# An RWKV-5 attention with a SoLU layer behind it: merged products from the fifth chunk on, and five smaller moves

## Chip, cores and metric

One core of a Trainium2 chip runs the program. Its engines are TensorE (PE, with its weight loads as PEld), VectorE (DVE), ScalarE (ACT), GpSimd (POOL) and SyncE (SP, which issues nearly all DMAs here). The metric is the device time of one execution in microseconds (us), as the median of several runs.

## The reference

For each batch b (4) and head h (8), over 768 steps with 48-long vectors, a state of 48x48 is carried; its result, laid out as 3072 rows (tokens) of 384, goes through a two-layer network whose middle is a softmax-weighted unit and a layer norm.

```python
for t in range(S):
    cur = einsum('bhd,bhe->bhde', u * k_t, v_t)
    y[:, :, t] = einsum('bhd,bhde->bhe', r_t, state + cur)
    state = w * state + einsum('bhd,bhe->bhde', k_t, v_t)
x = y as (4*768, 384)
h = x @ w_in                      # 384 -> 1024
solu = h * softmax(h)
ln = (solu - mean) / sqrt(var + 1e-6) * g_ln
out = ln @ w_out                  # 1024 -> 384
```

w_in, w_out and g_ln hold their values in 64 bits; the kernel makes 32-bit weights of them itself.

## The kernel before

**Chunks.** The 768 steps are cut into 6 chunks of 128, times 4 batches: 24 chunks, numbered so that chunk i+4 follows chunk i in the same batch (L461). Chunks 0 to 3 have no state before them. Everything stands in `direct_path`; each engine works its instructions in the order in which the code issues them, so the code's order is the order of each queue. (`general_path` runs only where a check of the inputs' ranges asks for it, and is not touched.)

**A chunk's way.** Loads of k, r and v (`load`). POOL multiplies k with decay factors (kp, `decay_k`, L701), and k, u and r with each other (`weigh`, L714 and L715); DVE sums that over each head (`sum_own`, L719). k and r must then be turned: up to chunk 8 by PE (`turn_r`, `turn_k`, L761 and L769, written out by DVE at L762 and ACT at L771), from chunk 9 on by a DMA transpose of 16-bit halves (`halve_rk`, copies on ACT L1008 and DVE L1013; `join_rk`, L990). Scores are products of turned k and r; the part above the diagonal is taken into a tile in SBUF (`take_scores`), whose diagonal was filled beforehand (`diagonal`). y is the product of v with that tile; `take_y` copies it to xT on ACT (L874). Outer products of kp and v renew the state.

**Whole and merged chunks.** Chunks below WHOLE (7) work on 128 steps at once: `whole_scores` (L784), a diagonal by eight ACT instructions (L729), `whole_y` (L841), which has a separate product with the state where there is one, and `whole_outer` (L899). From WHOLE on a chunk is cut into halves of 64: `scores` (L802), a diagonal by two POOL instructions (L734), `outer` (L890), and `merged_y` (L863), in which state and v lie in one tile (`vts`, planes 0 and 1) and the turned r is placed under the scores by four ACT copies (`place`, L754 and L755), so that one product makes both. That needs the state in the middle of the chunk (`middle`, DVE L911) and zeros in the gaps of the value tiles (POOL, L1132 and L1133) and of the score tiles (ACT, L750). `update` (DVE L925 and L927, POOL L930) writes the next state into the value tile of chunk i+4.

**The layer.** `ffn_in` (PE L940, then exp on ACT, L945, with row sums) fills a score bank pair `h_ps`, of which there is one; `unit` divides and multiplies (DVE L951, L953: the last reader of `h_ps`), shifts by the mean (ACT L955) and sums squares (`square`, ACT L962). `deviation` makes the factor 1/sigma on POOL (L967, L969), one chunk at a time. `halve_ln` (ACT L996), a DMA transpose (L985 on SP) and `join_ln` (DVE L990) turn the unit's output, and `ffn_out` (PE L1035, ACT L1037) makes the result.

**Weights.** Fourteen pieces are converted: `take_up` (ACT L530), `convert_b` (DVE L543, L545), `convert_c` (POOL L553), and for w_out `convert_d` (DVE L560).

**Order.** After a written-out start, iterations i = 2 to 6 (L1137 to L1178) each do one chunk of attention and, from 3 on, one chunk of the layer's first half (chunk j = i-2). Then comes a written-out first pair (i = 7, chunks 7 and 8; L1209 to L1257), and the loop over pairs (i = 9, 11, ...; L1259 to L1326), which does two chunks of attention (i, i+1), two of the first half (j, j+1) and two of the second half (l = i-7, l+1). PSUM has four banks (`psM`) for all products except scores and `h_ps`.

Of the kernel before, what the change touches and what calls it, by code (L numbers as in the profile page):

```python
# [399 lines left out]
def direct_path(  # L400
# [29 lines left out]
    nc = tc.nc  # L430
# [10 lines left out]
    LA, LO, FIRST, WHOLE = 2, 5, 9, 7  # L441
# [114 lines left out]
    def convert_d(j):  # L556
        dst, _, f = pieces[j]
        ma, low = step.pop(j)
        if f is not None:
            nc.vector.tensor_scalar_mul(out=dst, in0=ma.bitcast(F32),  # L560
                                        scalar1=minus_g[:, f : f + 1])
# [35 lines left out]
    def spin(n):  # L597

        ps = psH.tile([128, dff], F32, tag="h", name="spin")
        for _ in range(n):  # L600
            nc.tensor.matmul(ps[:, 0:128], ident, ident, start=True, stop=True)
# [8 lines left out]
    pairs = wpool.tile([128, 2, HP, 2, D], F32, tag="check", name="state", bufs=1)  # L610
    third = wpool.tile([128, HP, 2, D], F32, tag="mag", name="state", bufs=1)
    states = [pairs[:, 0], pairs[:, 1], third]
    for St in states:
        nc.scalar.activation(out=St.rearrange("p a q d -> p (a q d)"),
                             in_=ident[:, 0:1].to_broadcast([128, dm]), func=ACT.Copy, scale=0.0)

# [11 lines left out]
    nc.scalar.copy(out=u_bc.rearrange("p h d -> p (h d)"), in_=u_ps)  # L628
    spin(3)
# [35 lines left out]
    N = len(units)  # L665
    sums = const.tile([128, N], F32, name="sums")
# [79 lines left out]
    def place(i):  # L746

        X = live[i]
        if i < WHOLE + 4:
            nc.scalar.activation(out=X["G"][32:64, 1].rearrange("p a q u -> p (a q u)"),  # L750
                                 in_=ident[32:64, 0:1].to_broadcast([32, H * U]), func=ACT.Copy, scale=0.0)
        for q in range(2):
            rows = slice(q * P, q * P + D)
            nc.scalar.copy(out=X["G"][P : P + D, 0, :, q, :], in_=X["rT"][rows, :, 0:U])  # L754
            nc.scalar.copy(out=X["G"][0:D, 1, :, q, :], in_=X["rT"][rows, :, U:T])  # L755
# [33 lines left out]
    def scores(chunks):  # L789
        chunks = [i for i in chunks if i < N]  # L790
        if not chunks:
            return
        ps = [t.rearrange("p (n a t) -> p n a t", n=2, t=U) for t in banks]
        for n, i in enumerate(chunks):
            X = live[i]
            X["scores"] = [ps[q][:, n] for q in range(2)]
            X["scores_both"] = both_banks.rearrange("p q (n a t) -> p q n a t", n=2, t=U)[:, :, n]
            for a in range(HP):
                for c in range(2):
                    for q in range(2):  # L800
                        rows = slice(q * P, q * P + D)
                        nc.tensor.matmul(X["scores"][q][ts(c, U), a, :], X["kT"][rows, a, ts(c, U)],  # L802
                                         X["rT"][rows, a, ts(c, U)], start=True, stop=True)
# [27 lines left out]
    def whole_y(i):  # L831
        b, c = units[i]
        X = live[i]
        vt, AT, St = vts[i % NV], X["AT"], states[b] if c > 0 else None
        vf = vt[:, 0].rearrange("p h x -> p (h x)")
        y_ps = psM.tile([128, KD, 128], F32, tag="m", name="y_ps")
        opened = set()

        def into(m, lhsT, rhs, stop):
            j, g = divmod(m, 4)  # L840
            nc.tensor.matmul(y_ps[32 * g : 32 * g + 32, j, :], lhsT, rhs, start=(g not in opened),  # L841
                             stop=stop, skip_group_check=True)
            opened.add(g)

        if c > 0:
            for m in range(12):
                a, n = divmod(m, 3)
                into(m, St[:, a].rearrange("p q d -> p (q d)")[:, ts(n, 32)], X["rT"][:, a, :],
                     False)
        for n, (m, h, at) in enumerate(inner):  # L850
            into(m, vf[:, at : at + 32], AT[:, h, :], last[m] == n)
        X["y"] = [y_ps]
# [52 lines left out]
    def mid(i):  # L905
        return vts[i % NV][0:D, 1, :, 0:D].rearrange("p (a q) d -> p a q d", q=2)
# [7 lines left out]
    def update(i):  # L914
        b, c = units[i]
        if c == C - 1:
            return
        X = live[i]
        for q in range(2):
            rows = slice(q * P, q * P + D)  # L920
            wT = pw[rows, 0, 7].unsqueeze(2).to_broadcast([D, HP, D])
            old = mid(i)[:, :, q] if i >= WHOLE else states[b][rows, :, q] if c > 0 else None
            new = carried(i + B)[:, :, q] if i + B >= WHOLE else states[b][rows, :, q]
            if old is None:
                nc.vector.tensor_mul(new, X["kv"][rows], wT)  # L925
            else:
                nc.vector.tensor_add(new, X["kv"][1][rows] if i >= WHOLE else X["kv"][rows], old)  # L927
        if i >= WHOLE or c > 0:
            S = vts[(i + B) % NV][P : P + D, 0, :, 0:D]
            nc.gpsimd.tensor_mul(S, S, wide[P : P + D].unsqueeze(2).to_broadcast([D, H, D]))  # L930
# [16 lines left out]
    def unit(i, later=False):  # L947
        X = live[i]
        st = small.tile([128, 8], F32, name="st", bufs=LO + 3)
        rs, tot, ss, var, rstd = (st[:, n : n + 1] for n in range(5))  # L950
        nc.vector.reciprocal(out=rs, in_=sums[:, i : i + 1])  # L951
        solu = X["solu"] = fpool.tile([128, dff], F32, name="solu", bufs=LO)
        nc.vector.scalar_tensor_tensor(out=solu, in0=X["h"], scalar=rs, in1=X["e"],  # L953
                                       op0=ALU.mult, op1=ALU.mult, accum_out=tot)
        nc.scalar.activation(out=solu, in_=solu, func=ACT.Identity, scale=-float(dff), bias=tot)  # L955
        X["st"] = ss, var, rstd
        if not later:
            square(i)

    def square(i):  # L960
        X = live[i]
        nc.scalar.activation(out=X["e"], in_=X["solu"], func=ACT.Square, accum_out=X["st"][0])  # L962

    def deviation(i):
        ss, var, rstd = live[i]["st"]
        live[i]["rstd"] = rstd
        nc.gpsimd.tensor_scalar(out=var, in0=ss, scalar1=1.0 / dff, scalar2=1e-6 * dff ** 2,  # L967
                                op0=ALU.mult, op1=ALU.add)
        nc.gpsimd.tensor_tensor(out=rstd, in0=var, in1=neg_half, op=ALU.pow)  # L969

# [66 lines left out]


# [90 lines left out]
    for vt in vts:  # L1131
        nc.gpsimd.memset(vt[:, 1, :, D:], 0.0)  # L1132
        nc.gpsimd.memset(vt[32:64, 1], 0.0)  # L1133

    todo = list(range(6, len(pieces)))
    now = []
    for i in range(LA, LA + LO):  # L1137
# [5 lines left out]
        before, now = now, [todo.pop(0) for _ in range(2 if todo else 0)]  # L1143
        for p in before:
            convert_c(p)
        turn_r(i + 2)
        turn_k(i + 2)
        if i > LA:
            diagonal(i + 1)
            unit(j)  # L1150
        sum_own(i + 2)
# [4 lines left out]
        if 0 <= j - 1:  # L1156
            deviation(j - 1)
# [4 lines left out]
        halve_rk(i + 3)  # L1162
# [3 lines left out]
        if i > LA:  # L1166
            whole_y(i)
            take_y(i)
            whole_outer(i)
            update(i)  # L1170
        for p in now:
            take_up(p)
        if i == LA:
            nc.vector.tensor_single_scalar(out=minus_g, in_=g_sb, scalar=-1.0, op=ALU.mult)
        for p in before:
            convert_d(p)
        for p in now:
            convert_b(p)  # L1178

# [9 lines left out]

    def attend(chunks):  # L1190

        chunks = [i for i in chunks if i < N]
        scores(chunks)
        outer(chunks)

    def take(chunks):
        chunks = [i for i in chunks if i < N]
        for i in chunks:
            take_scores(i)
        for i in chunks:  # L1200
            middle(i)
# [12 lines left out]
    diagonal(i + 1)  # L1214
    ffn_in(j)
    halve_k(i + 3)
    attend([i, i + 1])
    unit(j)
    halve_r(i + 3)
    place(i)  # L1220
# [3 lines left out]
    take([i, i + 1])  # L1224
# [5 lines left out]
    for n in (j - 2, j - 1):  # L1230
        if LO - 1 <= n:
            deviation(n)
# [7 lines left out]
    unit(j + 1, True)  # L1240
    halve_rk(i + 4)
# [9 lines left out]
    square(j + 1)  # L1251
    halve_ln(l + 3)
    join_ln(l + 2)
    halve_rk(i + 5)
    place(i + 2)
    place(i + 3)
    sum_own(i + 5)  # L1257

    for i in range(LA + LO + 2, N + LA + LO, 2):  # L1259
# [11 lines left out]
        for n in (j - 2, j - 1):  # L1271
            if LO - 1 <= n < N:
                deviation(n)
# [3 lines left out]

        second_pair = i == LA + LO + 2
        if l + 2 < N and not second_pair:
            halve_ln(l + 2)  # L1280
# [3 lines left out]
        if j < N:  # L1284
            unit(j)
# [3 lines left out]
        take([i, i + 1])  # L1289
        if second_pair:  # L1290
            halve_ln(l + 2)
# [6 lines left out]
        if j + 1 < N:  # L1298
            ffn_in(j + 1)
            unit(j + 1, True)  # L1300
# [15 lines left out]
        if j + 1 < N:  # L1316
            square(j + 1)
# [52 lines left out]
```

## Time and profile before

| | us |
|---|---|
| three runs | 337.73, 337.31, 336.42 (median 337.31) |
| the profiled execution | 337.11, of it the span from first to last instruction 335.3 |
| busy: PE, DVE, ACT, POOL | 323.0, 222.9, 231.1, 203.1 |
| L940, 288 records (24 chunks) | 129.0 |
| L1035, 400 records (24 chunks) | 128.3 |
| waits of PE longer than 0.4 us from 20 us on | 1.09 at 39.47, 0.43 at 94.46, 2.00 at 121.28 |

Rows of the timeline give start, duration, engine, line, operation, tiles, number of instructions, and in brackets the idle time before them with what ended it. Every 32-bit product is two records. The granted clock of PE is 1.00 in all windows from 0 to 330 us. The mean duration of a line can mix instructions alone with those that ran beside another engine's.

### The profile page before, as it was taken

Reading aid. Unit: us, or ns where it says so; the run is one execution under the profiler, and the core shown is the slowest. Engines: PE = TensorE matmul, PEld = TensorE weight load, DVE = VectorE, ACT = ScalarE, POOL = GpSimd, SP = SyncE. Lnnn points to the kernel's source line nnn. Section 1 sums busy time; section 2 is a strip of 40 time slices with the busy share of each in tenths; the row PEclk is TensorE's granted clock in tenths of the full one; section 3 lists DMA queues with packets and bytes.
Section 4 is the critical chain, followed back from the end, with each engine's and each line's share of the span. In section 5 each row is a group of like instructions: output and inputs, shape, how many; then the busy total and the mean of one; then the engine's idle time right before and its main releaser. Section 6 shows DMA issues by size and latency. Waiting matters only on the chain.

```text
span 335.3 us, 9036 instructions
## 1 busy us (share of the span) xinstructions
PE 323.0 (96%) x3667; PEld 192.3 (57%) x3667; DVE 222.9 (66%) x381; ACT 231.1 (69%) x393; POOL 203.1 (61%) x231
## 2 busy tenths in 40 slices
PE   8989899999999979999999999999999999999993
PEld 6956566665556546556556556556465555555572
DVE  8796889887964993995965975956927606333410
ACT  3776787986797776777677587588688386457411
POOL 6799988799999989679599389494150000000000
PEclk9999999999999999999999999999999999999999
DMA  7999999289799999999999998769485525355531
GB/s 149 235 269 220 206 238 158 34 143 167 159 197 191 170 214 188 144 185 168 189 201 142 148 217 148 155 168 208 71 153 126 118 72 133 65 133 134 134 90 31
DMA packets 165008, 52.59 MB, mean 157 GB/s; under 512 B 158173, under 2 KB 161374, under 8 KB 164958
## 3 DMA queue, kind: packets, MB, share of 16 engines
q1 hardware_dynamic: 164956, 51.92, 84.3%
q8 instruction: 31, 0.51, 0.7%
q14 instruction: 19, 0.16, 0.2%
q10 hardware_dynamic: 2, 0.00, 0.0%
HBM read 26.75 MB, written 4.72 MB: 94 GB/s over the span
## 4 chain that ended last, share of the span: by engine, by line
PE 68%; POOL 16%; DVE 5%; issue 4%; ACT 3%; DMA 2%; POOLq 0%; DVEq 0%; ACTq 0%
PE o_ps L1035 31%; PE h_ps L940 27%; POOL kp L701 4%; PE y_ps L863 4%; POOL rku L715 2%; POOL rku L714 2%; PE at L802 2%; POOL big L734 2%; DMA halves<-halves 2%; POOL rp L708 1%; PE kv_ps L890 1%; DVE ma L545 1%; POOL vt L1133 1%; PE y_ps L841 1%; POOL w_in_sb L553 1%
## 5 line engine op out<-in xcount | busy, mean ns | idle before, releaser
L940 PE MATMUL h_ps<-w_in_sb,xT 128*128 128x512 f32 x288 | 129.0, 597 | 2.4 <-ACT xT L874 2.4
L1035 PE MATMUL o_ps<-w_out_sb,lnT 128*128 128x384 f32 (+1 forms) x400 | 128.3, 476 | 0.0
L1035 PEld LDWEIGHTS o_ps<-w_out_sb,lnT 128*128 128x128 f32 x400 | 74.3, 190 | 48.6 <-issue 3.8
L940 PEld LDWEIGHTS h_ps<-w_in_sb,xT 128*128 128x128 f32 x288 | 53.5, 190 | 64.1 <-issue 57.0
L955 ACT ACTIVATE solu<-solu,st 128x1024 f32<-128x1024 f32 x24 | 27.5, 1148 | 36.2 <-DVE solu L953 36.2
L996 ACT COPY halves<-solu 128x2048 uint16<-128x2048 uint16 x24 | 45.3, 1889 | 1.1 <-DMA halves<-halves 1.0
L990 DVE COPY lnT<-halves 128x2048 uint16<-128x2048 uint16 x24 | 37.7, 1572 | 7.0 <-DMA halves<-halves 7.0
L930 POOL TENSOR_TENSOR vt<-vt,wide 48x384 f32<-48x384 f32 x16 | 19.6, 1238 | 31.9 <-DVE vt L927 31.6
L967 POOL TENSOR_SCALAR st<-st 128x1 f32<-128x1 f32 x24 | 6.7, 277 | 52.5 <-ACT e L962 52.3
L945 ACT ACTIVATE e<-h_ps 128x1024 f32<-128x1024 f32 x24 | 24.5, 1020 | 17.8 <-PE h_ps L940 17.8
L701 POOL TENSOR_TENSOR kp<-kpad,kdec 128x512 f32<-128x512 f32 x24 | 33.3, 1391 | 2.4 <-ACT kdec L652 1.6
L951 DVE RECIPROCAL st<-sums 128x1 f32<-128x1 f32 x24 | 3.8, 160 | 43.8 <-ACT e L945 43.7
L734 POOL TENSOR_SCALAR_AFFINE_SELECT big<-own 64x512 f32<-64x512 f32 x34 | 31.2, 919 | 2.2 <-PE y_ps L863 0.2
L953 DVE SCALAR_TENSOR_TENSOR solu<-h_ps,st,e 128x1024 f32<-128x1024 f32 x24 | 30.8, 1284 | 2.1
L1037 ACT ACTIVATE o<-o_ps,st 128x384 f32<-128x384 f32 (+1 forms) x25 | 14.0, 560 | 22.7 <-PE o_ps L1035 14.8
L714 POOL TENSOR_TENSOR rku<-kpad,u_bc 128x384 f32<-128x384 f32 x24 | 28.0, 1167 | 1.7 <-ACT u_bc L628 1.7
L715 POOL TENSOR_TENSOR rku<-rku,rpad 128x384 f32<-128x384 f32 x24 | 26.3, 1097 | 1.9
L573 DVE TENSOR_REDUCE least<-mag 128x1 f32<-128x384 f32 (+1 forms) x14 | 8.5, 607 | 26.6 <-ACT mag L571 26.6
L962 ACT ACTIVATE e<-solu 128x1024 f32<-128x1024 f32 x24 | 25.4, 1060 | 0.5
L815 DVE COPY_PREDICATED big<-later_half,at 64x512 f32<-64x512 uint32 x34 | 25.0, 734 | 0.4
L990 DVE COPY big<-halves 128x2048 uint16<-128x2048 uint16 x15 | 23.4, 1562 | 0.3
L708 POOL TENSOR_TENSOR rp<-rpad,rdec 128x512 f32<-128x512 f32 x15 | 22.3, 1486 | 0.0
(105 smaller groups left out, 406.1 us busy)
## 6 DMA issues: line engine op xcount, KB each, us to landing
raw<-in_moe_w_in_dram SPq DMA_DIRECT2D x12, 512.0 KB, 5.1
raw<-in_moe_w_out_dram SPq DMA_DIRECT2D x16, 384.0 KB, 4.0
kpad<-in_k_dram SPq DMA_DIRECT2D x24, 192.0 KB, 4.8
rpad<-in_r_dram SPq DMA_DIRECT2D x24, 192.0 KB, 5.2
out_dram<-o SPq DMA_DIRECT2D x23, 192.0 KB, 3.4
vt<-in_v_dram SPq DMA_DIRECT2D x34, 96.0 KB, 4.0
vt<-in_v_dram SPq DMA_DIRECT2D x7, 192.0 KB, 6.2
halves<-halves SPq DMA_TRANSPOSE x39, 5.0
```

Of the source, the lines that this page charges most:

```text
L701: nc.gpsimd.tensor_mul(X["kp"].rearrange("p h d -> p (h d)"), kpads[i % NLD].rearrange("p h d -> p (h d)"), kdec.rearrange("p a d -> p (a ...
L708: nc.gpsimd.tensor_mul(X["rp"].rearrange("p h d -> p (h d)"), rpads[i % NLD].rearrange("p h d -> p (h d)"), rdec.rearrange("p a d -> p (a ...
L714: engine.tensor_mul(rku, kpads[i % NLD][:, :, 0:D], u_bc)
L715: engine.tensor_mul(rku, rku, rpads[i % NLD][:, :, 0:D])
L734: nc.gpsimd.affine_select(out=G[rows, c].rearrange("p a q u -> p (a q) u"), in_=X["own"][rows].to_broadcast([U, H, U]), compare_op=ALU.is_ ...
L940: nc.tensor.matmul(h_ps[:, ts(n, NX)], X["xT"][:, j, :], w_in_sb[:, j, ts(n, NX)], start=(j == 0), stop=(j == KD - 1))
L953: nc.vector.scalar_tensor_tensor(out=solu, in0=X["h"], scalar=rs, in1=X["e"], op0=ALU.mult, op1=ALU.mult, accum_out=tot)
L955: nc.scalar.activation(out=solu, in_=solu, func=ACT.Identity, scale=-float(dff), bias=tot)
L962: nc.scalar.activation(out=X["e"], in_=X["solu"], func=ACT.Square, accum_out=X["st"][0])
L990: nc.vector.tensor_copy(out=words.bitcast(U16).rearrange("p n (t o) -> p o n t", o=2), in_=turned)
L996: nc.scalar.copy(out=both.rearrange("p (o n) -> p o n", o=2), in_=split(X["solu"]))
L1035: nc.tensor.matmul(o_ps, X["lnT"][:, f, :], w_out_sb[:, f, part], start=(f == 0), stop=(f == KF - 1))
```

## The change

- WHOLE goes from 7 to 4: chunks 4, 5 and 6 are merged like the later ones. With it the state tiles of the whole chunks and their zeros go, `whole_y` loses its product with the state, and `update` always writes into the value tile of chunk i+4.
- The zeros of the value tiles' second plane are made by six ACT instructions at the start instead of twelve POOL memsets before the iterations; the zeros of the score tiles (L750) go.
- In iterations 3 to 6 the scores and outer product of the merged chunk i+1 come in iteration i, placed and with their middle state, as a single chunk; the first pair has these of chunk 8 alone.
- `unit` is two parts: `unit_a` (DVE) and `unit_b` (ACT: L955 and L962). In the pairs `unit_b` comes after other ACT work: for j after the halves of chunk l+2, for j+1 after the copies to xT.
- `deviation` takes several chunks at once: chunks 0 to 4 in the first pair, then two at a time.
- Of the scalings of w_out in the iterations (`convert_d`) the odd pieces go to ACT; `take_up` comes earlier in an iteration, and `convert_d` before the sums.
- `halve_rk` of chunk 9 moves to the end of iteration 6, of chunk 11 behind the first pair's xT, of chunk 12 into the pair i = 9, and so do the placing copies of chunks 9 and 10.

```diff
-    LA, LO, FIRST, WHOLE = 2, 5, 9, 7
+    LA, LO, FIRST, WHOLE = 2, 5, 9, 4
...
+    for vt in vts:
+        nc.scalar.activation(out=vt[:, 1].rearrange("p h x -> p (h x)"),
+                             in_=ident[:, 0:1].to_broadcast([128, H * P]), func=ACT.Copy, scale=0.0)
...
     def place(i):
-        if i < WHOLE + 4:
-            nc.scalar.activation(out=X["G"][32:64, 1]..., func=ACT.Copy, scale=0.0)
...
+    def unit_a(i):
         nc.vector.reciprocal(out=rs, in_=sums[:, i : i + 1])
         nc.vector.scalar_tensor_tensor(out=solu, in0=X["h"], scalar=rs, in1=X["e"], ...)
+    def unit_b(i):
         nc.scalar.activation(out=solu, in_=solu, func=ACT.Identity, scale=-float(dff), bias=tot)
+        nc.scalar.activation(out=X["e"], in_=solu, func=ACT.Square, accum_out=ss)
...
-    for vt in vts:
-        nc.gpsimd.memset(vt[:, 1, :, D:], 0.0)
-        nc.gpsimd.memset(vt[32:64, 1], 0.0)
...
     for i in range(LA, LA + LO):
         turn_r(i + 2)
         turn_k(i + 2)
         for p in before:
             convert_c(p)
+        for p in now:
+            take_up(p)
         if i > LA:
             diagonal(i + 1)
             unit(j)
+        for p in before:
+            convert_d(p, p % 2)
...
-        if 0 <= j - 1:
-            deviation(j - 1)
...
-        halve_rk(i + 3)
         if i + 1 < WHOLE:
             whole_scores(i + 1)
             take_scores(i + 1)
+        else:
+            place(i + 1)
+            attend([i + 1])
+            middle(i + 1)
-        if i > LA:
+        if LA < i < WHOLE:
             whole_y(i)
             take_y(i)
             whole_outer(i)
+        elif i >= WHOLE:
+            merged_y(i)
+            take_y(i)
+        if i > LA:
             update(i)
...
+        if i + 1 >= WHOLE:
+            take_scores(i + 1)
         for p in now:
             convert_b(p)
+        halve_rk(i + 3)
...
+    deviation(0, j)
     ffn_in(j)
     halve_k(i + 3)
-    attend([i, i + 1])
+    attend([i + 1], 1)
...
-    unit(j + 1, True)
-    halve_rk(i + 4)
+    unit_a(j + 1)
...
-    square(j + 1)
+    halve_rk(i + 4)
+    unit_b(j + 1)
     halve_ln(l + 3)
     join_ln(l + 2)
-    halve_rk(i + 5)
-    place(i + 2)
-    place(i + 3)
...
         if j < N:
             ffn_in(j)
         attend([i, i + 1])
         if j < N:
-            unit(j)
+            unit_a(j)
+        if second_pair:
+            place(i)
+            place(i + 1)
+        if l + 2 < N:
+            halve_ln(l + 2)
+        if j < N:
+            unit_b(j)
+        take([i, i + 1])
+        if second_pair:
+            halve_rk(i + 3)
```

`attend(chunks, at)` is `scores` and `outer` of those chunks; `at` says in which half of the score banks the first of them stands.

## The prediction

> **What bounds the kernel now.** I read the busy shares first, then the chain that ended last, then TensorE's timeline, and last the other engines' timelines where TensorE had waited.
>
> ```profile
> PE 323.0 (96%) x3667; PEld 192.3 (57%) x3667; DVE 222.9 (66%) x381; ACT 231.1 (69%) x393; POOL 203.1 (61%) x231
> PE 68%; POOL 16%; DVE 5%; issue 4%; ACT 3%; DMA 2%; POOLq 0%; DVEq 0%; ACTq 0%
> ```
>
> TensorE (PE) is busy 96% of the span, yet the chain that ended last is only 68% PE: for a third of the time something else sets when PE goes on. The timeline of PE says where:
>
> ```profile
> 39.47 0.66 PE L769 MATMUL tk_ps<-ident,kp 128*128 128x128 f32 x4 [1.09 <-POOL kp L701]
> ...
> 60.92 5.42 PE L940 MATMUL h_ps<-w_in_sb,xT 128*128 128x512 f32 x12
> ...
> 94.46 5.42 PE L940 MATMUL h_ps<-w_in_sb,xT 128*128 128x512 f32 x12 [0.43 <-ACT xT L874]
> ...
> 121.28 5.42 PE L940 MATMUL h_ps<-w_in_sb,xT 128*128 128x512 f32 x12 [2.00 <-ACT xT L874]
> ...
> 318.95 10.63 PE L1035 MATMUL o_ps<-w_out_sb,lnT 128*128 128x384 f32 x48
> ```
>
> After 121.28 PE has no wait to its last product at 329.6, in periods of 24.76 us a pair (121.28 to 146.04). So the change can move the end by what it takes from PE before 121.28, and no more, unless it puts a wait into the pairs. I follow the starts of the W_in products (L940) of chunks 2, 3, 4, 5, 6, 7 and 9: 42.42, 51.67, 60.92, 69.22, 81.62, 94.46 and 121.28.
>
> Between 57 and 121 the chain runs mostly through POOL, then ACT, a transpose and DVE, while PE waits only 2.4 us: those engines are as late as PE is. The timeline of ACT and of DVE in iteration 5 shows it:
>
> ```profile
> 57.19 1.03 ACT L945 ACTIVATE e<-h_ps 128x1024 f32<-128x1024 f32 x1 [1.83 <-PE h_ps L940]
> 58.66 2.46 ACT L729 ACTIVATE big<-ident,own 128x128 f32<-128x128 f32 x8
> 61.02 1.14 ACT L955 ACTIVATE solu<-solu,st 128x1024 f32<-128x1024 f32 x1
> 62.19 1.06 ACT L962 ACTIVATE e<-solu 128x1024 f32<-128x1024 f32 x1
> 63.24 1.88 ACT L996 COPY halves<-solu 128x2048 uint16<-128x2048 uint16 x1
> 66.43 1.03 ACT L945 ACTIVATE e<-h_ps 128x1024 f32<-128x1024 f32 x1
> ```
>
> From exp to exp ACT has 9.24 us of work and no gap: the last line has no bracket, it waited for nobody.
>
> **PE's own work.** A whole chunk with a state costs, start to start in iteration 4 (48.64 to 51.67), scores 1.02, state 0.68, y 0.88, outer 0.45: 3.03 us. For a merged chunk taken singly I use the last odd chunk: scores 0.51 (275.17 to 275.68), outer 0.47, y 1.04 (286.65 to 287.69): 2.02; its outer product has only one plane, but in pairs 64 and 32 records took the same 0.83, so records are not what it costs. Three chunks times 1.01 are 3.0 us. They fall so: iterations 4 and 5 1.0 each; iterations 3 and 6 nothing, since scores and outer product of the next chunk come an iteration earlier; the first pair 0.8, which has scores and outer of one chunk instead of two.
>
> **Waits on PE.** The 1.09 at 39.47 (1.26 by starts, 38.21 to 39.47) stands behind POOL's zeroing of the value tiles, 32.85 to 38.07, which goes: kp of chunk 5 is then ready near 34.2, before PE asks. Nothing is late next there: its loads were issued at 28.15 and land after 4.8 by the page's median.
>
> **Zeros on ACT.** Six fills of 128x512 follow the copy of u, which ends at 5.52; the next thing on ACT, kdec, starts at 9.23 after 3.71 us of waiting for PE. By the pitch of the 128x384 zeros (three in 1.35, 0.42 each) the six take 2.5, by that of the 32x512 zeros (81.79 to 82.44) 3.9. So it costs 0 to 0.2 on kdec, which releases POOL's first kp; I take 0.1. If the cover were gone, all 3.9 would land on POOL's chain.
>
> **Iterations 3 to 6, worked by the queues.** Per iteration DVE gains the two middle sums (L911, 0.35 each) and loses one of two scalings (L560, 0.39 to 0.94); scores taken in cost 1.46 against 1.36. ACT loses the diagonal (2.46) and gets four placing copies (0.40 each) and the odd scaling (0.55, by the 128x384 copies). POOL gains 2 x 0.69 for the diagonal and loses 0.19 + 0.55 and more for the deviation. Going through the new order with these durations:
> - Chunk 2's product can start at 41.05: PE's queue from 37.78 without the wait. That is 1.4 earlier.
> - Iteration 4: PE would be through at 49.3, but the product needs the score bank that unit (L953) reads last: exp 46.6 to 47.8, unit to 49.5. Start 49.6, 2.1 earlier.
> - Iteration 5: DVE ends its conversions at 55.9, turns r to 56.6, unit ends at 58.1; the outer product waits 0.3 for a PSUM bank behind that turn. Start 58.2, 2.7 earlier.
> - Iteration 6: ACT after 58.1 has L955 1.17, square 1.27, scaling 0.55, halves 1.90, placing 1.65, xT 0.47: 7.0, so exp of chunk 4 starts at 65.2, though PE was done at 63.45. Unit ends at 68.1. Start of chunk 5's product 68.15, only 1.1 earlier: ACT takes back 1.6.
> - First pair: scores of chunk 8 wait for chunk 7's to be taken (73.9, 0.5 late; same bank), then 0.8 less work: chunk 6's product at 80.15, 1.5 earlier. ACT has placing of chunk 7, halves of k 9 and chunk 1's halves before exp of chunk 5: 76.1 to 77.3; unit ends at 79.05, 1.1 us before PE needs it.
> - Then ACT is lighter: one chunk placed instead of two, and four 0.63 zeros gone over both pairs (before, placing and zeros ran 81.79 to 86.43). xT of chunk 7 no longer stands behind halves and L955: the 0.43 goes. Chunk 7's product at 92.5, 2.0 earlier.
>
> **The 2.00 at 121.28.** xT of chunk 9 (120.76) stood behind L955 of chunk 8, which waited 3.95 for DVE's unit at 117.92:
>
> ```profile
> 119.25 1.15 ACT L955 ACTIVATE solu<-solu,st 128x1024 f32<-128x1024 f32 x1 [3.95 <-DVE solu L953]
> ```
>
> DVE was late since exp of chunk 7 came at 103.42, 3.6 us after PE's end, behind eight placing copies and two zeros. In the new order exp of chunk 7 starts at 98.1 with placing behind it, unit of chunk 8 ends near 115, and L955 stands behind xT. PE needs the bank at 117.3. What is late next is the transposed chunk 3: its halves end at 98.1, the transpose took 5.9 (101.45 to 107.3), the join 1.8, so 106 to 108.3 against a need at 110. I count the 2.0 as gone: chunk 9's product at 117.3, 4.0 earlier.
>
> **Deviations.** 11 calls replace 24. Wide ones are not in the trace: for five columns the power costs between 0.55 (the narrow one) and 2.75 (five of it); I take 0.8, nearest to its mean of 0.816. POOL is 4 us ahead there by the memsets and the missing narrow ones, so even 2.75 does not reach PE. In the pairs, two columns against two calls: at most what it was.
>
> **The pairs.** Halves of chunk l+2 go behind exp, which starts earlier by that 1.9 and later by L955's 1.17; unit is due at 158.46 and would end near 155.8. No wait added.
>
> **Sum.** 4.0 earlier, less 0.1 for the zeros, is 3.9. The profiled execution was 337.11 (span 335.3 and 1.8 around it), so 333.2; the runs' median 337.31 lies 0.2 higher, which makes it 333.4.
>
> [...] The stretch of DVE is what the queues above assume least surely:
>
> ```profile
> L545 DVE SCALAR_TENSOR_TENSOR ma<-raw,ma x8: 559/560/1279, 36.4 to 65.5; 128x384 uint32<-128x384 uint32 x8
> ```
>
> One instruction takes 0.56 or 1.28 us, the long ones beside POOL's work. Eight of them at 1.279 instead of their mean 0.801 are 3.8 us more on DVE, in iterations where DVE is nearly full.
> By the timeline three of the eight were long (48.03, 55.01, 56.39), each beside a POOL instruction, and I take that share again.
> [...]
>
> **Rivals.** (1) PE never waits before 121: 1.26 + 3.0 (without the misses above) + 0.43 + 2.0 = 6.7, so 330.6. For it: POOL is ahead; against: ACT's full 9.24 us in iteration 5. [...] (3) Slower: the second kv tile of chunk i+1 now keeps a PSUM bank from one iteration to the next, with four banks in all. If y of chunk i is given the bank that the middle sums free, PE waits for DVE's middle (51.2 in iteration 4 against 48.2 wanted): 3 us in each of four iterations, 12 less the 3.9, about 345; two such iterations (6 less 3.9) already make it slower than before. Against it: the program before hands out banks in the order in which they are freed, and the turned k, copied by ACT at 48.3, is freed first.
>
> **Chances.** Forecast 0.62 (331.3 to 335.5), rival 1 0.12, rival 2 0.17, rival 3 0.09. Half a percent is about what a measurement of this kernel tells from no change: faster 0.74, same 0.17, slower 0.09. The range 330.6 to 337.2 leaves out rival 3, some of rival 2's end and half of rival 1.
>
> **What would show it.** Right: no PE wait at L769 near 38; L940 starts near 41, 49.6, 58.2, 68, 80, 92.5, 117; ACT gapless before the exp near 65; unit, not PE, behind the L940 waits. Wrong: PE waits at L863 on L911 (rival 3), L545 all at 1.28 (rival 2), or a wait at L1035 on the join of a transpose near 110.

## The result and the profile after

The changed kernel takes 340.95 us (median of four runs, 340.54 to 342.84); the kernel before took 337.27 beside it. The ratio is 1.0121, with an interval of 1.0084 to 1.0159: slower by 1.2%, where 333.4 was predicted and 330.6 to 337.2 given as the range. The profiled execution is the slowest of the four, 342.84 with a span of 340.7, so its trace holds about 2 us more than the median.

The page first: busy times, the chain that ended last by engine, and the granted clock in 40 slices.

```profile
PE 323.9 (95%) x3691; PEld 191.3 (56%) x3691; DVE 225.7 (66%) x383; ACT 231.4 (68%) x384; POOL 189.2 (56%) x199
PE 64%; POOL 11%; SPq 8%; DVE 5%; DMA 4%; issue 4%; ACT 1%; POOLq 0%; ACTq 0%; DVEq 0%
PEclk9999979999999989999999999999999999999999
```

PE is as busy as before, though it was to lose 3.0 us of work; half clock, below, hides what it lost (with both stalls mended, in e3, PE is busy for 320.8: 2.2 less than before, not 3.0). The chain shows something new: SP's queue (SPq) at 8%, which it did not name before. And the clock, 9 in every slice before, has a 7 and an 8. The timeline of PE says where:

```profile
41.76 0.26 PE L883 MATMUL kv_ps<-vt,kp 64*48 64x48 f32 x2 [2.13 <-DMA vt<-in_v_dram]
43.46 0.88 PE L883 MATMUL kv_ps<-vt,kp 64*48 64x48 f32 x30 [1.44 <-DMA vt<-in_v_dram]
...
46.63 5.42 PE L932 MATMUL h_ps<-w_in_sb,xT 128*128 128x512 f32 x12
...
124.92 7.08 PE L932 MATMUL h_ps<-w_in_sb,xT 128*128 128x512 f32 x12 [2.59 <-DVE solu L944]
...
324.24 10.63 PE L1025 MATMUL o_ps<-w_out_sb,lnT 128*128 128x384 f32 x48
```

The three old waits (1.09, 0.43, 2.00) are gone, as predicted; two new ones stand in other places: 3.57 us for a value tile near 41, and 2.59 for DVE's unit ahead of chunk 9's W_in product (L932, L940 before). The chain of waits in the window of the first one, each step released by the one above it:

```profile
34.74 1.29 POOL kp L702
...
36.08 3.40 SPq L478
39.48 0.05 issue
39.53 3.79 DMA vt<-in_v_dram
43.33 0.14 issue
43.46 0.88 PE kv_ps L883 x30
```

SP issues the two halves of chunk 4's v from 36.08 on, and the second lands at 43.33. The kernel before issued the same v at 35.96 and had no wait there, since it needed it one iteration later. Its row:

```profile
35.96 3.33 SPq L478 DMA_DIRECT2D vt<-in_v_dram  x1
```

The change brings chunk 4's outer product forward into iteration 3, and its v was not brought forward with it.

The second stall starts on ACT. Its timeline, and a row of SP's:

```profile
120.27 1.90 ACT L986 COPY halves<-solu 128x2048 uint16<-128x2048 uint16 x1 [3.84 <-DMA halves<-halves]
122.08 1.02 ACT L937 ACTIVATE e<-h_ps 128x1024 f32<-128x1024 f32 x1
```

```profile
112.25 3.28 SPq L478 DMA_DIRECT2D vt<-in_v_dram  x4
115.62 8.97 SPq L975 DMA_TRANSPOSE halves<-halves  x3
```

The copy of chunk 5's unit into halves waits 3.84 for one of the six buffers that halves and raw weights share. The transposes that would free one (of chunk 4's unit, and of chunks 12 and 13) are three in a row, some 3 us each, behind the loads of the next chunks. exp, behind that copy on ACT, comes at 122.08, the unit ends at 124.8, and PE waits.

Behind each of the two stalls the clock halves. Windows of the trace: from and to, length, busy time of PE, PEld, DVE, ACT and POOL, then the granted clock, the DMA share and GB/s:

```profile
43.00:46.40 3.40, 2.94 (x84) 2.75 (x88) 0.82 (x3) 3.32 (x8) 2.77 (x3) 0.50 1.35 229
46.80:52.00 5.20, 5.20 (x14) 2.28 (x15) 4.58 (x8) 0.07 (x1) 1.29 (x2) 1.00 1.08 238
...
125.00:128.20 3.20, 3.20 (x4) 1.40 (x5) 3.11 (x7) 3.14 (x5) 2.52 (x2) 0.50 1.06 286
```

So chunk 9's W_in product takes 7.08 instead of 5.42.

**Where the time went.** The starts of the W_in products cut the run into four stretches (from chunk 9 on the pairs follow each other without a wait, before and after). "Predicted" is what the prediction's starts give. The kernels of the experiments stand in the same table; it carries most of what follows. All in us, each from one profiled execution.

| kernel | chunk 1 to 2 | 2 to 6 | 6 to 9 | 9 to 23 | 1 to 23 |
|---|---|---|---|---|---|
| before | 9.90 | 39.20 | 39.66 | 171.67 | 260.43 |
| predicted | 8.53 | 39.10 | 37.15 | 171.67 | 256.45 |
| after | 13.91 | 38.54 | 39.75 | 173.32 | 265.52 |
| e1, v of chunk 4 early | 8.91 | 39.36 | 39.49 | 173.36 | 261.12 |
| e2, halving of 12 put back | 13.42 | 39.53 | 37.09 | 171.76 | 261.80 |
| e3, both | 9.13 | 39.40 | 37.09 | 171.65 | 257.27 |
| e4, idle products in the waits | 13.14 | 38.58 | 42.37 | 171.56 | 265.65 |
| e3b, outer 4 late, 12 put back | 9.15 | 39.75 | 37.09 | 171.65 | 257.64 |
| e5, e3 with the turn first | 8.63 | 39.12 | 37.35 | 171.67 | 256.77 |
| e6, before with zeros on ACT | 9.18 | 39.17 | 39.66 | 171.67 | 259.68 |
| e7, before with the later moves | 9.88 | 39.20 | 37.09 | 171.65 | 257.82 |
| e8, e1 with loads behind | 8.94 | 39.40 | 37.09 | 172.75 | 258.18 |
| after, once more | 12.51 | 39.51 | 40.79 | 173.31 | 266.12 |

After loses 4.01 in the first stretch, 0.09 in the third and 1.65 in the last, and wins 0.66 in the second: 5.09, which with a first start 0.20 later is the 5.3 by which the last product starts later.

### The profile page after: what moved, and what is told of

Its sections match the earlier page's. It is cut to its first block, busy times and chain, and to the rows that moved or that the text cites. A ratio compares the mean times of both kernels' runs of the same rounds, so it can differ in the third digit from the quotient of the medians.

```text
span 340.7 us, 9038 instructions
## 1 busy us (share of the span) xinstructions
PE 323.9 (95%) x3691; PEld 191.3 (56%) x3691; DVE 225.7 (66%) x383; ACT 231.4 (68%) x384; POOL 189.2 (56%) x199
## 4 chain that ended last, share of the span: by engine, by line
PE 64%; POOL 11%; SPq 8%; DVE 5%; DMA 4%; issue 4%; ACT 1%; POOLq 0%; ACTq 0%; DVEq 0%
PE o_ps L1025 31%; PE h_ps L932 25%; PE y_ps L856 4%; SPq L478 3%; POOL big L735 3%; SPq L473 3%; POOL kp L702 3%; POOL rp L709 2%; PE at L800 2%; SPq L519 2%; DMA kpad<-in_k_dram 2%; PE kv_ps L883 2%; POOL rku L715 2%; DMA halves<-halves 1%; DVE solu L944 1%
## 5 line engine op out<-in xcount | busy, mean ns | idle before, releaser
L932 PE MATMUL h_ps<-w_in_sb,xT 128*128 128x512 f32 x288 | 130.9, 604 | 2.6 <-DVE solu L944 2.6
L1025 PE MATMUL o_ps<-w_out_sb,lnT 128*128 128x384 f32 (+1 forms) x400 | 128.3, 476 | 0.0
L932 PEld LDWEIGHTS h_ps<-w_in_sb,xT 128*128 128x128 f32 x288 | 54.1, 192 | 65.5 <-issue 58.0
L1027 ACT ACTIVATE o<-o_ps,stats 128x384 f32<-128x384 f32 (+1 forms) x25 | 14.1, 563 | 40.1 <-PE o_ps L1025 27.1
L735 POOL TENSOR_SCALAR_AFFINE_SELECT big<-own 64x512 f32<-64x512 f32 x40 | 36.1, 903 | 2.2
L942 DVE RECIPROCAL stats<-sums 128x1 f32<-128x1 f32 x24 | 3.9, 162 | 47.6 <-ACT e L937 47.4
L960 POOL TENSOR_SCALAR stats<-stats 128x2 f32<-128x2 f32 (+2 forms) x11 | 3.8, 341 | 53.2 <-ACT e L952 53.1
L944 DVE SCALAR_TENSOR_TENSOR solu<-h_ps,stats,e 128x1024 f32<-128x1024 f32 x24 | 30.8, 1284 | 2.1
L951 ACT ACTIVATE solu<-solu,stats 128x1024 f32<-128x1024 f32 x24 | 27.6, 1149 | 5.6 <-DVE solu L944 5.5
L813 DVE COPY_PREDICATED big<-later_half,at 64x512 f32<-64x512 uint32 x40 | 29.5, 738 | 0.7
L715 POOL TENSOR_TENSOR rku<-kpad,u_bc 128x384 f32<-128x384 f32 x24 | 26.1, 1087 | 1.6 <-ACT u_bc L625 1.6
L856 PEld LDWEIGHTS y_ps<-big,vt 128*32 128x32 f32 (+1 forms) x1280 | 18.5, 110 | 5.4 <-issue 5.1
```

Source lines behind the costliest of these rows:

```text
L715: engine.tensor_mul(rku, kpads[i % NLD][:, :, 0:D], u_bc)
L735: nc.gpsimd.affine_select(out=G[rows, c].rearrange("p a q u -> p (a q) u"), in_=X["own"][rows].to_broadcast([U, H, U]), compare_op=ALU.is_ ...
L813: nc.vector.copy_predicated(X["G"][rows, c].rearrange("p a q u -> p q a u"), later_half[rows].unsqueeze(1).to_broadcast([U, 2, HP, U]), X[ ...
L856: nc.tensor.matmul(y_ps[ts(g, 32), j, ts(c, U)], vf[:, at : at + 32], X["G"][rows, c, h // 2, h % 2, :], start=(g not in opened), stop=las ...
L932: nc.tensor.matmul(h_ps[:, ts(n, NX)], X["xT"][:, j, :], w_in_sb[:, j, ts(n, NX)], start=(j == 0), stop=(j == KD - 1))
L1025: nc.tensor.matmul(o_ps, X["lnT"][:, f, :], w_out_sb[:, f, part], start=(f == 0), stop=(f == KF - 1))
```

## The experiments

Two theories of the stalls: (A) chunk 4's outer product asks for v too early; (B) moving chunk 12's halving into the second pair puts its transposes where they hold up the buffers. The first four runs shared a chip with the kernel before (336.16).

**e1**: v of chunk 4 is loaded one step earlier.

```diff
     load(5, "kr")
+    load(4, "v")
     load(3, "v")
...
     load(6, "kr")
-    load(4, "v")
```

> The changed kernel with one load moved: v of chunk 4 is issued just ahead of v of chunk 3 instead of behind k and r of chunk 6. Theory A (the outer product of chunk 4, asked for an iteration earlier than before, finds its v not landed: PE waits 2.13 + 1.44 at L883 and then runs 2.6 us at half clock): the wait falls to about 1 us (v of chunk 3 may be late instead), no half clock near 45, and the end comes 3 to 4 us earlier, 337 to 338. Rival (the merged form loads VectorE so much in iterations 3 to 6 that the wait on v only covers a wait on VectorE): PE waits for L944 or L760 instead, the end stays within 1 us of 341.

Measured: 339.37, ratio 1.0093 (1.0062 to 1.0124). The first stretch falls from 13.91 to 8.91, with the clock at 1.00 from 38 to 50; the second stall stays, 2.33, with half clock behind it. The wait on v is gone altogether, more than the 1 us that was expected to stay; the end comes 1.6 earlier by the medians, not 3 to 4. These medians are of two separate measurements, and the changed kernel's runs differ (its second measurement, below), so the gain is read from the traces.

**e2**: chunk 12's halving goes back to the end of the first pair.

```diff
     join_ln(l + 2)
+    halve_rk(i + 5)
...
-        if second_pair:
-            halve_rk(i + 3)
```

> The changed kernel with one part undone: the halves of k and r of chunk 12 are made at the end of the first pair again, not in the pair i = 9. Theory B (three transposes in a row on SyncE's queue in that pair keep all six halves buffers taken, ScalarE's halves of chunk 5 wait 3.84 for one, exp of chunk 8 comes 7 us after its product and PE waits 2.59 for the unit, then runs 3 us at half clock): no wait of L986 on a transpose near 120, no wait of PE at 124.9, the end 4 us earlier, about 337. Rival (SyncE is simply late there, whatever the order): the transpose moved ahead delays the loads and the next transposes, the wait at 124.9 stays above 1.5, the end within 1 us of 341.

Measured: 339.11, ratio 1.0078 (1.0049 to 1.0107). The other half of the picture: the third stretch falls to 37.09 and chunk 9's product has no wait, while v is waited for as in the changed kernel (2.45 and 0.38).

**e3**: both edits.

> The changed kernel with both edits, v of chunk 4 issued ahead of v of chunk 3 and the halves of chunk 12 back in the first pair. If A and B are separate and together the whole loss: the two gains add, 333 to 334, below the kernel before (337.3). If one of them only uncovers the other, or VectorE and ScalarE bound iterations 3 to 6 anyway: 336 to 338.

Measured: 334.78, a little above the 333 to 334 of separate causes; ratio 0.9941 (0.9916 to 0.9967), the clock 1.000 throughout. Where two lines stand is worth 1.8% by the ratios of this run and of the change (2.5% by the change's second measurement, below), and the rest of the change is a gain of 0.6%. PE's timeline, with what is left over:

```profile
42.49 5.42 PE L932 MATMUL h_ps<-w_in_sb,xT 128*128 128x512 f32 x12
49.95 0.57 PE L883 MATMUL kv_ps<-vt,kp 64*48 64x48 f32 x30 [0.47 <-DVE big L760]
51.49 5.42 PE L932 MATMUL h_ps<-w_in_sb,xT 128*128 128x512 f32 x12
...
118.98 5.42 PE L932 MATMUL h_ps<-w_in_sb,xT 128*128 128x512 f32 x12
```

Chunk 9's product, predicted at 117.3, starts at 118.98. Of these 1.7, 0.84 are the first W_in product's, which starts at 33.36 (32.52 to 33.70 in the runs, for reasons not followed up); the other 0.84 is what stays of waits of 0.5 to 0.7 for DVE's turn L760, one in each iteration. The outer product (L883) doesn't read the turned r: it waits for the PSUM bank that L760 empties.

**e4**: is the half clock a cost of its own? PE gets idle products to do in the two waits: 17 ahead of chunk 4's outer product, 11 ahead of chunk 9's W_in product, into a tile that nobody reads.

```diff
+    def turns(n):
+        ps = psM.tile([128, 128], F32, tag="m", name="turns")
+        for _ in range(n):
+            nc.tensor.matmul(ps, ident, ident, start=True, stop=True)
...
+        if chunks == [WHOLE]:
+            turns(17)
...
+            if i == LA + LO + 4:
+                turns(11)
```

> The changed kernel with products added that nobody reads: 17 of 128x128 between the scores and the outer product of chunk 4, and 11 ahead of the product with W_in of chunk 9, so that PE works through both waits. The waits themselves stay. If the half clock after each wait (0.54 from 44.0 to 46.6, 0.50 from 125 to 128) comes of PE standing idle: the clock stays 1.00, about 1.0 and 1.7 us less, 338 to 339. If the clock falls for another reason: 341 or above, with the same slices at half clock.

Measured: 342.26, ratio 1.0171 (1.0121 to 1.0221): a miss as a whole, for a reason that PE's timeline shows.

```profile
39.60 4.06 PE L610 MATMUL turns<-ident 128*128 128x128 f32 x34
43.84 0.79 PE L888 MATMUL kv_ps<-vt,kp 64*48 64x48 f32 x32 [0.17 <-DMA vt<-in_v_dram]
...
124.30 2.72 PE L610 MATMUL turns<-ident 128*128 128x128 f32 x22 [2.66 <-ACT o L1032]
```

In the first place they filled the wait, the clock stayed at 1.00, and chunk 2's product came 0.73 sooner than in after, though the wait on v ended 0.38 later (43.84 against 43.46): the half clock's price there is 0.7 at the least, 1.1 counted from the end of that wait. In the second place they waited for a PSUM bank themselves and came after the wait: 2.6 lost. The clock did not halve there (1.00 in every window from 116 to 130), though PE had been idle for 2.66. What this says of the clock is taken up at the end.

The next four shared a chip with the kernel before at 336.27.

**e3b**: theory A without touching a load: scores of chunk 4 stay in iteration 3, its outer product and middle state go back to iteration 4; chunk 12's halving is put back as in e2.

```diff
+        if i == WHOLE:
+            outer([i])
+            middle(i)
...
-            attend([i + 1])
-            middle(i + 1)
+            scores([i + 1])
+            if i + 1 > WHOLE:
+                outer([i + 1])
+                middle(i + 1)
```

> The changed kernel with the outer product and the middle state of chunk 4 put back into iteration 4 (they run in iteration 3 in the changed kernel) and with the halving of chunk 12 put back into the first pair; no transfer is issued at another place than in the changed kernel but chunk 12's transposes. Theory A (what was lost is that chunk 4's outer product asks for v of chunk 4 one iteration before it has landed): the wait of the outer product on vt near 42 is gone with no load moved, no half clock behind it, W_in's product of chunk 2 starts near 42.5 instead of 46.63, and the time is that of the kernel in which v was loaded earlier, 334 to 335.5. Rival (it was the order of the loads on SP's queue, and not the earlier asking, that the kernel with the early v mended): the wait moves to another load and 338 to 339.5 stays.

Measured: 335.10, ratio 0.9970 (0.9955 to 0.9984). No wait on v, 9.15 in the first stretch: A holds, the order of the loads was not needed to explain it.

**e5**: e3, and the second of each two pieces of w_out is split by DVE after the next unit instead of before the next turn.

```diff
-        for p in before:
+        for p in before[:1]:
             convert_c(p)
...
             unit(j)
+        for p in before[1:]:
+            convert_b(p)
+            convert_c(p)
...
-        for p in now:
+        for p in now[:1]:
             convert_b(p)
```

> The kernel with v of chunk 4 early and the halving of chunk 12 put back, with one edit: of the two pieces of w_out that each of the iterations 2 to 5 takes up, the second is split (L543, L545 on DVE) after the next iteration's unit instead of before its turn. Theory D (in iterations 4 to 6 the start of W_in's product is set by DVE's order: the turn L760 comes late behind L545's 1.28, the outer product waits 0.47 to 0.67 for that turn, and L942 and L944 come after it): those waits go, each of the iterations 4 and 5 takes 8.5 to 8.7 instead of 9.0 to 9.2, W_in's product of chunk 5 starts near 68.7 instead of 69.90, and the whole is 0.5 to 1.5 shorter than that kernel, 333.3 to 334.3. Rival (the chain h, exp, unit is itself 8.9 to 9.2 long, or POOL's work is what ends last): the outer product no longer waits, W_in's product waits instead, and the time stays within 0.5.

Measured: 333.76, ratio 0.9938 (0.9915 to 0.9962). Chunk 5's product starts at 68.39 (68.7 expected, 69.90 in e3). The first iterations go as the theory has it, 8.63 and 8.54; the following ones wait 0.51 for chunk 6's v and 0.26 for L760, and the first pair gives 0.5 back. By the traces 1.3 are won up to chunk 5 and 0.5 are left at the end; the two ratios to before overlap, so that the times don't show even that. It is the lowest time of all runs.

**e6**: the kernel before, with only the zeros of the value tiles moved to ACT.

```diff
+    for vt in vts:
+        nc.scalar.activation(out=vt[:, 1]..., func=ACT.Copy, scale=0.0)
...
-    for vt in vts:
-        nc.gpsimd.memset(vt[:, 1, :, D:], 0.0)
-        nc.gpsimd.memset(vt[32:64, 1], 0.0)
```

> The kernel before with one edit: the zeros of the six value tiles are written by ScalarE early instead of by POOL's memsets ahead of iteration 2. By the prediction the wait of 1.09 for kp of chunk 5 at the turn near 39 goes, nothing is late next, and 1.1 to 1.3 are gained: 335 where the kernel before has 336.2. Theory now (the start of W_in's product of chunk 2 was 42.42 before and 42.49 where the changed kernel's wait for v is mended, so that the wait's end is given back): the wait at the turn goes, but chunk 2's product starts less than 0.4 earlier, and the whole is within 0.5 of the kernel before.

Measured: 335.91, ratio 1.0001 (0.998 to 1.0023). The wait at the turn goes, 0.72 of it show in the first stretch, and the times show nothing: between the two expectations, nearer to the second. Where the rest went stands in the timelines of DVE and POOL:

```profile
36.61 1.24 DVE L545 SCALAR_TENSOR_TENSOR ma<-raw,ma 128x384 uint32<-128x384 uint32 x1
37.77 1.15 DVE L543 TENSOR_SCALAR ma<-raw 128x384 uint32<-128x384 uint32 x1
38.96 1.24 DVE L545 SCALAR_TENSOR_TENSOR ma<-raw,ma 128x384 uint32<-128x384 uint32 x1
40.12 0.68 DVE L765 TENSOR_TENSOR big<-tr_ps,tab 128x512 f32<-128x512 f32 x1
```

```profile
36.13 1.31 POOL L717 TENSOR_TENSOR rku<-kpad,u_bc 128x384 f32<-128x384 f32 x1
37.51 1.19 POOL L718 TENSOR_TENSOR rku<-rku,rpad 128x384 f32<-128x384 f32 x1
38.67 1.11 POOL L553 TENSOR_TENSOR ma<-ma,low 128x384 uint32<-128x384 uint32 x1
```

In the kernel before, the same two conversions took 0.56 each, beside memsets:

```profile
36.45 0.56 DVE L545 SCALAR_TENSOR_TENSOR ma<-raw,ma 128x384 uint32<-128x384 uint32 x1
36.62 0.52 POOL L1133 MEMSET vt<- 32x512 f32 x1
37.38 0.56 DVE L545 SCALAR_TENSOR_TENSOR ma<-raw,ma 128x384 uint32<-128x384 uint32 x1
37.55 0.52 POOL L1133 MEMSET vt<- 32x512 f32 x1
```

With the memsets gone, POOL's products stand under them, and they take 1.24: the turn (L765) comes 1.7 later than there, at 40.12 instead of 38.41 (0.65 of this since the first W_in product started that much later in this run), and W_in waits 0.51 for the unit behind it. The wait changed hands.

**e7**: the kernel before with its seven whole chunks and POOL's zeros, and only the edits behind the seventh chunk: unit in two parts, deviations together, chunk 11's halving behind xT, chunks 9 and 10 placed in the second pair (the change's own lines for these); chunk 12's halving stays where it was.

> The kernel before, all seven first chunks whole and the zeros on POOL, with the edits to what follows the seventh chunk alone: unit in two parts with the second behind xT, deviations of five and two chunks at once, chunk 11's halving behind xT, placing of chunks 9 and 10 moved into the second pair; chunk 12's halving stays in the first pair. Theory B (the whole gain of the mended kernel, 2.3 by the start of chunk 9's product, is made here, and the merged chunks 4 to 6 give nothing): waits of 0.43 and 2.00 for xT gone, W_in's product of chunk 9 starts near 119 instead of 121.28, and the ratio to the kernel before is 0.993 to 0.995, that of the mended kernel. By the prediction's own terms, 3.0 of PE's work in iterations 4 to 6 carry through as well, and these edits alone give less than the mended kernel by 0.5 to 1.5.

Measured: 334.78, ratio 0.9957 (0.9942 to 0.9972). Chunk 9's product starts at 119.26, and the third stretch is 37.09, e3's to the hundredth. The whole of its 2.57 is made here. What e3 has beyond it, 0.75 less in the first stretch and 0.20 more in the second, is what the zeros alone gave (e6: 0.72) and a small loss for merging.

The last two shared a chip with the kernel before at 336.49.

**e8**: is it the queue, or are six buffers too few for the moved halving? e1, with the second pair's loads behind chunk 12's transposes instead of ahead.

```diff
+        def loads():
+            for n in (i + 6, i + 7):
...
+                    load(n, "v")
+        if i > LA + LO + 2:
+            loads()
...
         if second_pair:
             halve_rk(i + 3)
+            loads()
```

> The changed kernel with v of chunk 4 loaded one step earlier (as in the run that mended that wait, 1.009 to the kernel before), and with the second pair's loads (k and r of chunks 15 and 16, v of 12 and 13) issued behind the transposes of chunk 12 instead of ahead of them; chunk 12 is still halved in the second pair, where the change put it. Theory B1 (the second stall comes from the queue: the transposes of chunk 4's unit, chunk 12 and chunk 13 stand behind 6.4 of load issues on SP, and so the six halves buffers come free late): ScalarE's wait of 3.60 to 3.84 for a halves buffer near 116 to 120 is gone, W_in's product of chunk 9 starts near 119, 37.1 to 37.4 after chunk 6's, and the ratio is 0.993 to 0.997. Rival B2 (chunk 12's and 13's halves in one pair are too many for six buffers wherever the loads stand): the wait of 2 to 4 stays and the ratio is 1.006 to 1.011. Third: the loads come too late for chunk 12's v or chunk 15's k, and a wait on vt or kpad appears in the third pair.

Measured: 335.75, ratio 0.9973 (0.9948 to 0.9998). ACT's copy of chunk 5's halves does not wait any more, and the third stretch is 37.09 with chunk 12's halving where the change put it. So six buffers are enough for the moved halving once the transposes don't stand behind the loads: it is the queue. (With the loads ahead, one halving less is enough too, as e2 shows.) Something else is now late, 1.1 in the last stretch; the rows are ACT's and PE's:

```profile
113.14 1.89 ACT L986 COPY halves<-solu 128x2048 uint16<-128x2048 uint16 x1
```

```profile
127.32 5.40 PE L1025 MATMUL o_ps<-w_out_sb,lnT 128*128 128x384 f32 x16 [0.97 <-DVE lnT L980]
```

**The changed kernel once more**, since the single repairs and the double one did not add up in the medians.

> The changed kernel itself once more. The two mended kernels and the doubly mended one say that the stalls cost 4.3 and 4.6 of median, which would put it at 1.021 of the kernel before; its four runs gave 1.012, while its profiled run, the slowest of them, was 5.7 above the kernel before, as its trace accounts for. If the costs add up in every run, the ratio is 1.017 to 1.022 here; if runs differ in how much of the half clock behind each stall they take, it is 1.010 to 1.015 and the single runs lie 2 to 3 apart.

Measured: 343.95 (341.28 to 345.06, six runs), ratio 1.0193 (1.0145 to 1.024). Within the first expectation by ratio, and the single runs differ by more than the second one asked for. In this trace the second stall is larger:

```profile
126.34 7.00 PE L932 MATMUL h_ps<-w_in_sb,xT 128*128 128x512 f32 x12 [3.63 <-DVE solu L944]
```

By the traces the repairs do add up: e1 saves 4.40 of the distance from chunk 1 to 23, e2 3.72, both 8.25. How much of each stall and of the half clock a run takes differs from run to run.

## Why the prediction was wrong

- **The step that failed first** is in "PE's own work": iterations 3 and 6 were costed at nothing, "since scores and outer product of the next chunk come an iteration earlier". I moved the instructions and asked what they cost, not what they read. v of chunk 4 was issued at 35.96 in the trace of before and was needed in iteration 4; the new order needs it near 39.6. The row was there, and the page of before gives these loads 6.2 from issue to landing (median of seven whole v), which makes 42.2. Price: 4.8 in the first stretch (after against e3), 0.7 to 1.1 of it the half clock by e4; the second stretch gives 0.9 back.
- **The second** is in "The 2.00 at 121.28". That wait went, and the search for what is late next stopped at the transposed chunk 3 and found it in time. The moved `halve_rk(12)` was not followed past the loads of the second pair on SP's queue, nor were the six buffers counted. Price: 2.66 in the third stretch (after against e3), 1.66 of half clock behind it.
- **The zeros**: the wait of 1.09 went, but "nothing is late next there" was wrong. I asked for kp's loads; next was DVE's turn, behind two conversions that took 0.56 each beside memsets (before) and 1.24 beside POOL's products (e6). The term of 1.26 measures 0.72 (e6). Ahead of that, the cost on ACT was right: kdec starts at 9.23 in both.
- **The long conversions.** I took three long ones in eight, the share before. In after five in eight are long (1.25 to 1.29; e3 five, e6 four, before three). L545 took 0.56 beside memsets (before, 36.45 and 37.38) and 1.24 beside POOL's products (e6, 36.61 and 38.96): what ran on POOL beside DVE changed, and the share with it. That all eight would be long, 3.8 more and the upper end of the range, no run shows, and the sign of rival 2, L545 all at 1.28, did not come. The 0.6 missing in e3's first stretch goes with the long ones (e5, where one of the two conversions ahead of the turn is moved, has 8.63 against 8.53 predicted); they did not make the slowdown.
- **Iterations 4 to 6** (chunk 2 to 6): predicted 39.10, e3 39.40, before 39.20. That PE's own work saved there (2.2 by busy time, where 3.0 was said) would be eaten by DVE and ACT was right in size, and partly for another reason: each iteration waits 0.5 to 0.7 for the bank behind the turn, a wait that the prediction had at 0.3 and in iteration 5 alone, and not 1.6 once for ACT. That the sum comes out so near is in part luck.
- **The later moves**: 37.15 predicted for chunk 6 to 9, 37.09 in e3 and e7. Of all terms the best: the 0.43 and the 2.00 go by the later moves (e7 does not part the split unit from the later placing), and they need no merged chunk.
- **Deviations**: five columns took 1.20 in the power, against 0.8 taken and bounds of 0.55 and 2.75; it reached nothing. The pairs got no wait, as said.
- **Rivals.** Rival 3 (PSUM banks held by the next chunk's outer product) did not happen: y (L839, L856) waited on no middle sum. A PSUM bank was waited for, but the one that held the turned r. The slower side came by another way, and of the signs listed under "wrong" none was a wait on a load. The rivals looked at banks and engines; the two places that decided were a queue and a landing time.

With the two repairs the forecast's 333.4 compares with 334.78 (e3), 333.76 with the turn first (e5). These times flatter it, since the kernel before was 1.0 to 1.1 lower beside them: by ratio 0.988 was forecast, and both measured 0.994. From chunk 1 to 23, by the traces, 3.98 was forecast, and e3 won 3.16, e5 3.66; their first W_in product starts 0.8 and 0.6 later than in the one trace of before, and whether that is the change's doing stays open.

## What to carry to other kernels

An instruction that is moved ahead takes the deadlines of all that it reads with it: for each operand, look up when it lands in the trace of before, and compare with the new start. When a DMA moves in a queue's order, write down what it now stands behind and which buffers wait for it, as one would for an engine. And where an engine that ran short instructions beside another one is given its freed time for real work, its neighbour's durations need not be those of the trace: here L545's 0.56 (before) became 1.24 (e6).

## What the runs showed of the hardware

- **The half clock came in steps.** Seen in windows of 0.2 us a granted clock of 0.50 lasted 3.4 us each time (in after 43.0 to 46.4 and 124.9 to 128.3; in the repeated run 44.3 to 47.7 and 126.2 to 129.6; in e1 121.1 to 124.5), twice that in e2 (42.2 to 49.1). Its two starts are 81.9 apart in after and in the repeated run: 24 times 3.41. Some 2.2 of idle stood just ahead of the step in e1 and e2. Yet 2.00 (before, at 121.28) and 2.66 (e4) dropped nothing. That the steps lie on a grid of 3.41, and that where an idle time falls on it decides, is an estimate from these numbers alone; by the prices above it would make equal stalls differ by 0.7 to 1.7 from run to run. It was not tried by itself.
- **DVE beside POOL's memsets and beside its products.** L545 took 0.56 beside memsets (before, 36.45 and 37.38), as it did with POOL idle (before, 64.62; after, 49.45), and 1.24 beside products of two tiles (e6, 36.61 and 38.96). L543, with one input, took 1.15 there (37.77), and 0.36 and 0.43 beside memsets (before, 36.05 and 36.92).
- **What held SP's queue.** One chunk's v held it for 3.3 to 4.3 between 29 and 40 us (L478; 4.26 and 3.33 before, 4.11 and 4.08 in after), three transposes for 8.97. In after, the loads ahead of the three transposes held it from 109.12 to 115.53, and the transposes followed at 115.62.
